# SyncE joins the engines whose order is the written one, in an expert stage of seven block products

## The chip, the cores and the metric

One core of a Trainium2 chip runs the kernel. The metric is the device time in microseconds of one execution, as the median over runs. TensorE, VectorE (DVE), ScalarE (ACT), GpSimd (POOL) and SyncE (SP) each work off a queue of instructions in order. SyncE computes nothing here: it issues most of the DMAs.

## The reference

An attention without softmax feeds a mixture of 16 experts in 4 groups:

```python
scores = scale * np.matmul(z, z.transpose(0, 2, 1))      # u, v: 8 x 1856 x 256, z: 8 x 1856 x 64
attn = np.maximum(scores, 0.0) ** 2
x = (u * np.matmul(attn, v)).reshape(B * S, D)           # 14848 tokens
# each token: the best group by x @ w_group, the best of its 4 experts by x @ w_expert[g]
h = np.maximum(xg[mask_e] @ w1[g, e], 0.0)               # 256 -> 1024
out[tok_idx] = (g_w * e_w)[:, None] * (h @ w2[g, e])     # 1024 -> 256
```

All of it is computed to nearly float32 accuracy: each operand is split in a high and a low part, and each product is three matmuls.

## The kernel before

The attention takes the first 900 us and is not touched. Its tokens are written into a table in DRAM, `bucket`, sorted by expert. The experts are then taken in the order of their load. The first four are computed in the plain way. The last twelve, numbers 4 to 15, are computed each in two halves of at most 512 tokens, which share weights: phase 1 (`x @ w1`) uses seven block products where the plain way has eight. This stage runs from about 957 us to the end, and the change touches it alone.

For one expert `e` the program writes down this work:

- The product loop: 28 products of phase 1 (`step`, matmuls at L1318), 4 of which run already in the phase 2 of the expert before. With 20 left it calls `duo_rows(e + 1)`, which asks for the next expert's tokens: two register loads on SyncE for the expert's number and row (`regs`, L742 and L743), two transposing DMAs from `bucket` into `xp_w` (L1240), and two small loads of `meta_w` (L1247), the tokens' weights and places. With 8 left it calls `duo_w1(e + 1)`, two loads of 512 KB into the buffers `r0` and `r1` (L1182). Between products GpSimd splits this expert's `w2` out of the same two buffers (L1227, L1228).
- Phase 2 of the first half, `phase2_t(f"w{e}_0", ...)`: 48 matmuls (L871) in two sweeps. By the plan `A`, ScalarE and VectorE meanwhile split the next expert's `w1` (L1194, L1204, L1208 to L1211), then `duo_w2(e + 1)` loads its `w2` into `r0` and `r1` (L1188), then VectorE joins the next expert's tokens out of `xp_w` (L1261). At the end of each sweep ScalarE moves the result from PSUM to `yp_w` (L874, L879). At the end SyncE issues four transposing DMAs from `yp_w` to `yr_w` (L884).
- Phase 2 of the second half, `phase2_t(f"w{e}_1", ...)`, in the same way. By the plan `B`, the first four products of the next expert run among its matmuls, beginning in the second sweep (`1 11 go; 1 12 m; ...`). Among them is product 1, which ScalarE copies from PSUM to `duo_y` (L1336); products 6 and 2 are added on top.
- A result is sent by tiles of 128 tokens: a copy out of `yr_w` by ScalarE (L906) or VectorE (L910), a multiplication with the token's weight (L908, L913), and an indirect DMA by GpSimd (L914). The letters `sa`, `sv` in the plans and `send_part` in the product loop say when. By `B`, the two first tiles of an expert's first half are sent at `1 3 sv` and `1 8 sa`, in the second sweep of its second half, ahead of `1 11 go`.

Buffers: `xp_w` has 2, `meta_w` 7, `yr_w` 4, `yp_w` 2.

What sets the order: the program text is traced, and a scheduler arranges each engine's queue from it, unless told otherwise. Inside `tc.manual_schedule(engines=...)` the engines named keep the order in which the text was written. Around the twelve experts it names TensorE, ScalarE and VectorE. SyncE and GpSimd are arranged by the scheduler there: an instruction of a later expert may stand ahead of one of an earlier expert. Each instruction still waits for its data and buffers. The region opens before the first of the twelve experts' product loops and closes before the last half of the last one.

Of the kernel before, what the change touches and what calls it, by code (L numbers as in the profile page):

```python
# [29 lines left out]
def tile_glu_attn_moe(  # L30
# [1401 lines left out]
    while unsent:  # L1432
        unsent.pop(0)()
    in_order = ExitStack()
    in_order.enter_context(tc.manual_schedule(
        engines={mybir.EngineType.PE, mybir.EngineType.Activation, mybir.EngineType.DVE}
    ))
    sending = []

# [141 lines left out]
```

## Time and profile before

| | us |
|---|---|
| median of 3 runs | 1445.79 (1445.42 to 1455.44) |
| the profiled execution's own time | 1446.41 |
| its span, first to last instruction | 1444.5 |
| TensorE busy | 1420.8 (98%) |
| VectorE busy | 1214.9 (84%) |
| ScalarE busy | 1052.2 (73%) |
| GpSimd busy | 441.6 (31%) |

The clock column of a table of stretches is TensorE's granted clock as a share of full speed, a mean over the stretch. Matmuls are pipelined, so TensorE counts as busy also where it isn't at its peak. A row in a timeline gives the start, the time taken, the engine, the line of the program, the operation, what was written and read, and, in square brackets, how long the engine was idle just before and what ended that.

### The profile page before, as it was taken

How to read it: one execution, taken by the hardware profiler on the slowest of the kernel's cores; microseconds unless marked ns; L12 is line 12 of the kernel's file. 1: busy time of each engine (PE TensorE's matmuls, PEld its weight loads, DVE VectorE, ACT ScalarE, POOL GpSimd, SP SyncE). 2: the span in 40 equal slices, each digit the busy share in tenths (PEclk: the TensorE clock that was granted, in tenths of full speed). 3: DMA queues.
4: the chain of work that ended last, by engine and by line, in shares of the span. 5: the costliest groups of instructions: out<-in, count | busy, mean ns of one | idle time of the engine just before them, and what ended most of it. 6: DMA issues, size and time to landing. Idle time of an engine off the chain costs nothing.

```text
span 1444.5 us, 22598 instructions
## 1 busy us (share of the span) xinstructions
PE 1420.8 (98%) x6981; PEld 1227.3 (85%) x6981; DVE 1214.9 (84%) x2434; ACT 1052.2 (73%) x1850; POOL 441.6 (31%) x462
## 2 busy tenths in 40 slices
PE   9999999999999999999999999999999999999997
PEld 7898888888888888888788999978788888888896
DVE  7889999999998999989988578787787788678783
ACT  8897888787878878878775344456677777677674
POOL 0002012220222202221114222242445555555564
PEclk9999999999999999999999999999999999999999
DMA  9987969979699798995975464635444545545441
GB/s 320 336 236 210 253 169 258 235 212 225 178 261 227 195 235 189 263 235 149 247 184 154 95 184 77 148 86 120 119 120 111 136 121 129 131 133 131 121 116 52
DMA packets 400045, 256.47 MB, mean 178 GB/s; under 512 B 244132, under 2 KB 355263, under 8 KB 399921
## 3 DMA queue, kind: packets, MB, share of 16 engines
q1 hardware_dynamic: 387984, 223.97, 62.9%
q0 software_dynamic: 11856, 30.90, 6.9%
q8 instruction: 55, 0.90, 0.3%
q14 instruction: 70, 0.57, 0.1%
q10 hardware_dynamic: 80, 0.13, 0.0%
HBM read 108.29 MB, written 89.21 MB: 137 GB/s over the span
## 4 chain that ended last, share of the span: by engine, by line
PE 83%; DVE 9%; issue 3%; DMA 2%; ACT 2%; POOL 1%; SPq 0%; POOLq 0%; DVEq 0%; ACTq 0%
PE o L403 14%; PE o L404 14%; PE o L406 13%; PE yT L871 7%; PE duo_p L871 7%; PE duo_y L1318 5%; PE sc L366 5%; PE sc L367 5%; PE ph L794 2%; PE ph L795 2%; PE ph L796 2%; PE duo_x L1318 2%; PE duo_w L1318 2%; PE duo_p L1318 2%; DMA yr_w<-yp_w 2%
## 5 line engine op out<-in xcount | busy, mean ns | idle before, releaser
L403 PE MATMUL o<-ah,vl 128*128 128x512 f32 (+2 forms) x960 | 354.4, 370 | 0.6 <-DVE ah L378 0.4
L404 PE MATMUL o<-ah,vh 128*128 128x512 f32 (+2 forms) x960 | 354.3, 369 | 0.0
L406 PE MATMUL o<-al,vh 128*128 128x512 f32 (+2 forms) x896 | 329.0, 369 | 0.0
L638 POOL DMA_INDIRECT bucket<-rows,di x121 | 137.5, 1137 | 376.0 <-issue 216.6
L370 ACT ACTIVATE r<-sc 128x512 f32<-128x512 f32 (+2 forms) x312 | 178.7, 573 | 82.7 <-PE sc L367 77.7
L403 PEld LDWEIGHTS o<-ah,vl 128*128 128x128 f32 x960 | 180.2, 188 | 30.8 <-DVE ah L378 0.8
L914 POOL DMA_INDIRECT out_dram<-y_w,meta_w x92 | 148.6, 1615 | 188.8 <-ACT y_w L908 167.0
L404 PEld LDWEIGHTS o<-ah,vh 128*128 128x128 f32 x960 | 180.2, 188 | 29.0
L381 DVE TENSOR_TENSOR al<-r,ah 128x512 fp32r<-128x512 f32 (+2 forms) x280 | 187.9, 671 | 17.3 <-DVE ah L378 0.5
L406 PEld LDWEIGHTS o<-al,vh 128*128 128x128 f32 x896 | 167.9, 188 | 26.6 <-DVE al L381 0.7
L871 PE MATMUL duo_p<-hh_w,duo_w 128*128 128x496 f32 (+9 forms) x692 | 182.2, 377 | 0.0
L377 ACT ACTIVATE r<-r 128x512 f32<-128x512 f32 (+2 forms) x284 | 173.9, 612 | 9.0
L871 PEld LDWEIGHTS duo_p<-hh_w,duo_w 128*128 128x128 f32 x692 | 130.7, 189 | 17.3
L378 DVE CAST ah<-r 128x512 fp32r<-128x512 f32 (+2 forms) x284 | 117.7, 414 | 22.0 <-ACT r L377 15.1
L366 PE MATMUL sc<-zm,z2h 128*128 128x512 f32 (+2 forms) x312 | 120.1, 385 | 0.4 <-ACT vh L289 0.4
L367 PE MATMUL sc<-zm,z2l 128*128 128x512 f32 (+2 forms) x312 | 118.9, 381 | 0.0
L871 PE MATMUL duo_p<-hl_w,duo_w 128*128 128x496 f32 (+9 forms) x346 | 105.9, 376 | 0.0
L306 DVE STREAM_TRANSPOSE mt<-r 128x512 f32<-128x512 f32 x147 | 103.7, 705 | 0.6
L356 DVE TENSOR_TENSOR al<-at,ah 128x512 fp32r<-128x512 f32 (+1 forms) x168 | 95.3, 579 | 3.1 <-ACT ah L355 3.0
L355 ACT CAST ah<-at 128x512 fp32r<-128x512 f32 (+1 forms) x168 | 86.1, 532 | 7.7 <-DMA sym<-mt 4.6
L871 PE MATMUL yT<-hh,w_e 128*128 128x512 f32 (+6 forms) x384 | 83.3, 333 | 0.0
L914 POOL DMA_INDIRECT out_dram<-y,meta x37 | 40.8, 1104 | 120.7 <-DVE y L913 116.8
(237 smaller groups left out, 2862.1 us busy)
## 6 DMA issues: line engine op xcount, KB each, us to landing
sym<-mt SPq DMA_DIRECT2D x126, 256.0 KB
duo_r<-in_w_dram SPq DMA_DIRECT2D x48, 512.0 KB
at<-sym SPq DMA_DIRECT2D x84, 256.0 KB
bucket<-padrow SPq DMA_DIRECT2D x32, 660.0 KB
at<-sym SPq DMA_DIRECT2D x84, 160.0 KB
vr<-in_v_dram SPq DMA_DIRECT2D x23, 512.0 KB
ut<-in_uT_dram SPq DMA_DIRECT2D x23, 512.0 KB
raw_e<-in_w_dram SPq DMA_DIRECT2D x16, 512.0 KB
```

What stands on the lines that cost most here:

```text
L366: held(nc.tensor.matmul(ps[:, 0:w], z2h[:, ks], zm, start=True, stop=False))
L367: held(nc.tensor.matmul(ps[:, 0:w], z2l[:, ks], zm, start=False, stop=True))
L370: held(nc.scalar.activation(out=a, in_=ps[:, 0:w], func=AF.Relu, scale=1.0 / S))
L377: held(nc.scalar.activation(out=a, in_=a, func=AF.Square))
L381: held(nc.vector.tensor_sub(out=al, in0=a, in1=f32(ah)))
L403: held(nc.tensor.matmul(o, vl[:, dsl], ah, start=(i == 0), stop=False))
L404: held(nc.tensor.matmul(o, vh[:, dsl], ah, start=False, stop=end and al is None))
L406: held(nc.tensor.matmul(o, vh[:, dsl], al, start=False, stop=end))
L638: nc.gpsimd.indirect_dma_start(out=views[(b * NQ + 2 * half + hs[h]) * NT + i], out_offset=bass.IndirectOffsetOnAxis(ap=di[0:n, i0 + i:i0 ...
L871: nc.tensor.matmul(o, wt["2"][f // 2][:, w0:w0 + P], hs[f][q // 2][:, 0:n], start=(at == 0), stop=(at == 3 * NF - 1))
L914: nc.gpsimd.indirect_dma_start(out=outs(), out_offset=bass.IndirectOffsetOnAxis(ap=meta[0:m, t, 1:2], axis=0), in_=y[0:m], in_offset=None, ...
L1318: nc.tensor.matmul(out, a, b, start=(q == 0 and m in (1, 5)), stop=(q == 2), skip_group_check=True)
```

## The change

SyncE is named too. No instruction, buffer or size is changed.

```diff
@@ -1433,7 +1433,7 @@
         unsent.pop(0)()
     in_order = ExitStack()
     in_order.enter_context(tc.manual_schedule(
-        engines={mybir.EngineType.PE, mybir.EngineType.Activation, mybir.EngineType.DVE}
+        engines={mybir.EngineType.PE, mybir.EngineType.Activation, mybir.EngineType.DVE, mybir.EngineType.SP}
     ))
     sending = []
```

## Rows read from the trace of the kernel before

**Rows 1.** The page, section 1: engine, busy us, share of span, instructions.

```profile
PE 1420.8 (98%) x6981; PEld 1227.3 (85%) x6981; DVE 1214.9 (84%) x2434; ACT 1052.2 (73%) x1850; POOL 441.6 (31%) x462
```

**Rows 2.** Stretches, one per expert: length, engines' busy us, clock; ten and their sum.

```profile
1017.70:1062.00 44.30, 42.31 (x181) 34.80 (x180) 32.94 (x51) 30.30 (x50) 19.95 (x18) 0.96 0.48 118
...
1220.70:1264.00 43.30, 40.48 (x181) 35.88 (x181) 31.48 (x51) 29.09 (x50) 21.54 (x18) 0.92 0.51 117
...
1340.50:1379.80 39.30, 37.40 (x183) 34.99 (x181) 30.19 (x51) 27.85 (x50) 22.05 (x18) 0.96 0.50 130
1379.80:1415.30 35.50, 35.50 (x181) 33.73 (x180) 30.92 (x51) 28.23 (x50) 22.11 (x17) 1.00 0.34 94
sum 397.60, PE 387.47 PEld 341.15 DVE 316.91 ACT 291.04 POOL 215.96; mean PE 38.75 PEld 34.11 DVE 31.69 ACT 29.10 POOL 21.60
```

**Rows 3.** Waits of TensorE, 957 to 1444 us: total us, times, longest.

```profile
PE duo_y L1318 <- ACT duo_y L1336: 10.1, 7, 2.8
```

**Rows 4.** Timeline of ScalarE, 1351 to 1363 us, expert 13's phase 2.

```profile
1352.67 0.26 ACT L879 COPY yp_w<-duo_p 128x112 uint16<-128x112 uint16 x1
...
1357.39 0.26 ACT L879 COPY yp_w<-duo_p 128x112 uint16<-128x112 uint16 x1
1360.67 0.76 ACT L906 COPY y_w<-yr_w 128x512 uint16<-128x512 uint16 x1 [3.02 <-DMA yr_w<-yp_w]
...
1361.88 0.50 ACT L1336 COPY duo_y<-duo_x 128x424 f32<-128x424 f32 x1
```

**Rows 5.** Timeline of TensorE, the matmul behind that copy.

```profile
1362.43 0.92 PE L1318 MATMUL duo_y<-duo_x,duo_t 128*128 128x424 f32 x3 [1.90 <-ACT duo_y L1336]
```

**Rows 6.** Timeline of SyncE's queue, 1346 to 1380 us: issues, their time on the queue.

```profile
1346.80 2.55 SPq L1188 DMA_DIRECT2D duo_r<-in_w_dram  x2
1349.69 4.15 SPq L1247 DMA_DIRECT2D meta_w<-bucket  x2
1354.04 2.11 SPq L1240 DMA_TRANSPOSE xp_w<-bucket  x1
1356.26 5.14 SPq L884 DMA_TRANSPOSE yr_w<-yp_w  x4
1361.58 1.44 SPq L1240 DMA_TRANSPOSE xp_w<-bucket  x1
1367.47 5.42 SPq L884 DMA_TRANSPOSE yr_w<-yp_w  x4
1373.15 5.08 SPq L1182 DMA_DIRECT2D duo_r<-in_w_dram  x2
```

**Rows 7.** Waits of SyncE's queue, 957 to 1400 us: total us, times, longest.

```profile
SPq L1182 <- POOL duo_w L1228: 60.2, 12, 8.1
SPq L1247 <- DMA out_dram<-y_w,meta_w: 28.3, 9, 3.6
```

**Rows 8.** Timelines, 1392 to 1400 us, expert 14: SyncE's queue, ScalarE, VectorE, TensorE.

```profile
1392.00 40.50 SPq L884 DMA_TRANSPOSE yr_w<-yp_w  x12
...
1396.95 0.79 ACT L906 COPY y_w<-yr_w 128x512 uint16<-128x512 uint16 x1
...
1395.18 3.63 DVE L1194 TENSOR_TENSOR duo_x<-duo_r,duo_x 128x448 fp32r<-128x448 f32 x4
...
1399.09 0.77 PE L1318 MATMUL duo_y<-duo_x,duo_t 128*128 128x448 f32 x3
```

**Rows 9.** Register loads of an expert's number: ns min/median/max, first and last start.

```profile
L742 SPq TENSOR_LOAD <-eli x16: 262/269/496, 727.1 to 829.1; - x16
L742 SPq FUSED_REGOPS  x16: 147/147/187, 727.7 to 829.4; - x16
```

**Rows 10.** DMA, 1373 to 1385 us, 40 slices of 0.3 us; then ScalarE, VectorE.

```profile
GB/s 277 101 0 82 82 137 137 123 273 410 396 260 191 96 0 0 0 0 0 109 137 273 218 259 341 205 205 0 0 55 0 0 27 0 0 0 0 0 0 0
...
1381.36 0.62 ACT L1204 CAST duo_p<-duo_r 128x512 fp32r<-128x512 f32 x1
...
1382.72 0.69 DVE L1209 TENSOR_TENSOR duo_r<-duo_r,duo_r 128x512 f32<-128x512 f32 x1
```

## The prediction

> **What bounds the kernel now.** I read the page first, then the last third of the span by expert, then the waits of TensorE there, then the queue that feeds the engine it waits for.
>
> The page: TensorE is busy for 98% of the span [rows 1]. So a change pays only where it removes time in which TensorE stands still or runs slowly. The change touches the last stage alone (from about 957 us on), the experts computed by seven block products.
>
> The table by expert shows how much that is. Ten stretches, each from one expert's first output matmul to the next expert's, make 397.60 us, and TensorE is busy for 387.47 of them: 10.1 us idle [rows 2]. In three stretches the granted clock falls below 1.00, to 0.96, 0.92 and 0.96; in the other seven it is 1.00, as in the last one shown. The clock has two levels, 2.4 and 1.2 GHz, so a mean of 0.92 over 43.30 us means 3.5 us lost; the three together lose 0.04 x 44.30 + 0.08 x 43.30 + 0.04 x 39.30 = 6.8 us. The two with the longest waits are among them. The stage thus loses 10.1 + 6.8 = 16.9 us.
>
> The waits give one cause for all of the idle time: the matmul of L1318 into `duo_y` waits for ScalarE's copy L1336, 10.1 us in 7 waits, at most 2.8 [rows 3]. That copy itself takes 0.50 us. It is late because ScalarE's order is fixed and a copy of L906 stands ahead of it, which waited 3.02 us for a DMA, the transposes of `yr_w`; ScalarE had been free since 1357.65 [rows 4]. TensorE got its operand at 1362.43, after 1.90 us without work [rows 5].
>
> Why is that DMA late? The order of SyncE's queue tells [rows 6]. The `yr_w` transposes (L884) begin at 1356.26. Their input was complete at 1352.93, when the eviction L879 of the first half ended [rows 4]; that is 3.3 us earlier. Ahead of them stand two `meta_w` loads (4.15 us) and one `xp_w` transpose (2.11 us), which belong to the expert after next. The loads are long because they wait for scatters: 28.3 us in 9 waits [rows 7], 3.1 on average.
>
> **The change part by part.** It adds SyncE to the engines kept in the written order. No instruction is added or removed. In the written order, per expert, the queue holds `w1` (L1182), `w2` (L1188), `yr` of the first half, `yr` of the second half (L884), and then, in the next expert's product loop, `xp` twice (L1240), `meta` twice (L1247), and that loop's `w1`. Against rows 6, the two `meta` and two `xp` move from around the first `yr` to behind the second `yr`, ahead of `w1`. Also, the two register loads of `regs` (L742, L743), which now all run before 830 us [rows 9], come into the stage, ahead of the first `xp`.
>
> *What it gives.* The first `yr` starts when its input is there, 3.3 us earlier for the expert of rows 4 and 6. The trace has this case already: the expert whose `yr` starts at 1392.00 has no later expert's rows to fetch, so its queue is in the written order. There L906 runs at 1396.95 with no idle time before it, the matmul starts at 1399.09 with none either, and its stretch, the last of the ten, has clock 1.00 and no idle time [rows 2, 8]. It is also the shortest stretch, 35.50 us, with the least work of TensorE to hide behind. So I take all of the 10.1 us, and with them the 6.8 us of clock, as the clock fell only in stretches with such a wait: -16.9.
>
> *What the moved instructions cost in the new place.* The `xp` rows are first read by L1261, which the plan puts behind the whole split of `w1`, so they have more room than `w1` behind them, and that sets the price. Its delay per expert: register loads 2 x (0.27 + 0.15 + 0.02), about 1.1 with the gaps [rows 9]; `xp` 2.11 + 1.44 [rows 6]; two `meta` without the wait 4.15 - 3.1 = 1.0; gaps of about 0.2 each, 0.7: sum 6.3 us. The tightest is the last expert: the first `w1` load is issued at 1373.15, its bytes have come by about 1376.8 (the slices from the fourth to the thirteenth), and it is first read at 1381.36, 4.5 us later; the second has come at about 1381.1 (the twenty-seventh slice) and is read at 1382.72 [rows 6, 10]. Delayed by 6.3, the first lands at about 1383.1, 1.7 late. The second is held today not by the queue but by GpSimd, which must have read the buffer (L1182 waits for L1228, 5.0 us on average [rows 7]); it follows the first at the 400 GB/s of the fullest slices [rows 10], 512 KB in 1.3 us, and lands at about 1384.4, 1.7 late. VectorE then runs on without a pause to the matmul of 1399.09, with 0.28 us to spare (1395.18 + 3.63 against 1399.09) [rows 8]. So the last expert loses about 1.5 us. Wider experts have longer product loops and so more room: the first stretch without its idle time and clock loss is 44.30 - 1.99 - 1.77 = 40.5 us, against 35.5 for the last [rows 2]. I take nothing for them. The bounds: 0, if the loads overlap better, and 10 x 1.5 = 15 us, if all are as tight as the last. I take 1.5, as only the last has so little slack.
>
> The Trainium skill puts the floor of such a register load at about 0.6 us (DMA: Bandwidth & Descriptors, section Latency and other measured facts). The rows show a median of 0.27 [rows 9], so the trace is lower; by the page the delay of `w1` would be 0.7 us longer and the sum 0.7 us worse.
>
> What would have covered the wait of `meta`: by the new place the scatters it waited for are an expert's half older, so I cost it at nothing; if that cover is gone it costs what the second rival says. The order of TensorE, ScalarE and VectorE is fixed before and after. GpSimd's is not, and may be arranged anew; the rows give no sign of which way.
>
> *Sum.* 1446.4 (the profiled execution; span 1444.5) - 16.9 + 1.5 = 1431.0. The median of the runs shown is 0.6 us lower, which makes 1430.4; I say 1430.
>
> **Rivals.**
>
> 1. *Weight loads late for all.* `w1` slips past its slack in every expert, not only the last. For it: second loads that already land 1.6 us before their reader [rows 10]. Against: the wider experts' longer loops. Price: 10 x 1.5 = 15 us, so 1446.4 - 16.9 + 15 - 0.6 = 1444. The Trainium skill says that on each DMA engine descriptors are consumed in ring order (DMA: Bandwidth & Descriptors, section Queues, rings and completion order); by that, `w1` would also wait for the bytes of `xp` ahead of it, and this rival would come true. No row here shows `w1` behind `xp`.
>
> 2. *A new wait (the one that ends slower).* The `meta` loads keep their wait for a scatter in the new place, at 3.1 us, and `w1` queues behind them. The delay is then 9.4 us, and each of ten experts starts its weight work about 3.1 us late: 31 us, and if each wait costs clock as the three of rows 2 do (6.8 / 3 = 2.3), 23 more. On the sum above, 1430.4, that gives 1461 to 1484. It decides from a delay of about 8 us on. For it: 9 such waits today. Against: the buffers come from a set of seven, two per expert, and the scatters of the expert before last are over by then.
>
> 3. *The transposes stay late.* `yr` starts earlier but lands no sooner, as the second `w2` load is still moving when it starts, and half of the wait and of the clock loss stays: 1446.4 - 8.5 - 0.6 + 1.5 = 1439. Against: rows 8, where `w2` stands directly ahead too.
>
> 4. *The order hardly changes*, or TensorE finds another wait at the same place: 1446. Rows 6 are not the written order, so something must move; and rows 3 name no second cause.
>
> **How the numbers follow.** Forecast 0.60 (1427 to 1434), rival 1: 0.14, rival 2: 0.07, rival 3: 0.13, rival 4: 0.06. A measurement of this kernel can tell about 1% from no change, which is 14.5 us; the border is 1431.3. The forecast lies just past it, so I give 0.51 to faster (most of the forecast's 0.60), 0.42 to within 1% (the rest of it and rivals 1, 3 and 4), and 0.07 to slower. The lower end is 1427: all of the 16.9 with nothing lost is 1428.9, and the clock column's rounding (0.005 of 126.9 us) and its edges may hide a microsecond or two. The upper end, for 8 in 10, is 1442: it takes in the forecast and rival 3, and leaves out rivals 2 and 4 and most of 1.
>
> **What would show it.** Right: in SyncE's queue `yr_w` of the first half directly behind `w2`; no wait of L1318 for L1336; ScalarE's L906 with no idle time ahead of it; granted clock 1.00 in all ten stretches. The cost would show as a wait of ScalarE's L1204 or VectorE's L1208 or L1209 for the DMA of `duo_r`, in the last expert or two. Wrong: such waits from the first experts on, a wait of L1247 ahead of L1182, or a `duo_y` wait that stays.

## The result, and the profile after

The changed kernel takes 1436.11 us (median, 1435.32 to 1438.14), the kernel before 1447.63 us in the same measurement. The ratio is 0.9917, with a 95% interval of 0.9896 to 0.9939: 11.5 us or 0.8% faster, against a forecast of 16. That is inside the range and on the right side, but just under the 1% that the prediction took as the border. Among the executions of the kernel before that were measured with the first four experiments, one took 1554.99 us at a granted clock of 0.85; the ratios leave it out, and 1443.08 us below is the median with it (1442.25 without).

The profiled execution took 1438.14 us, with a span of 1436.1; it is the slowest of the seven. I compare it with that of before in the order of the prediction.

**The queue.** SyncE's queue for the same stretch as [rows 6] (start us, time on the queue, operation, count):

```profile
1338.50 2.55 SPq L1188 DMA_DIRECT2D duo_r<-in_w_dram  x2
1344.51 15.55 SPq L884 DMA_TRANSPOSE yr_w<-yp_w  x8
1361.40 3.89 SPq L1240 DMA_TRANSPOSE xp_w<-bucket  x2
1365.63 1.11 SPq L1247 DMA_DIRECT2D meta_w<-bucket  x2
1367.00 0.94 SPq L1182 DMA_DIRECT2D duo_r<-in_w_dram  x2
```

It is the written order: `w2`, both halves' `yr`, `xp`, `meta`, `w1`. The `meta` loads take 1.11 us instead of 4.15. The price stands in the same rows: the last `yr` ends at 1344.51 + 15.55 = 1360.06, and `w1` is issued at 1367.00, 6.9 us later. Before, it followed after 0.3 [rows 6].

**The wait that was to go.** ScalarE and TensorE at the place of [rows 4, 5] (the first copy ends the first half, whose `yr` are then issued):

```profile
1344.38 0.26 ACT L879 COPY yp_w<-duo_p 128x112 uint16<-128x112 uint16 x1
...
1349.24 0.80 ACT L906 COPY y_w<-yr_w 128x512 uint16<-128x512 uint16 x1
...
1350.49 0.51 ACT L1336 COPY duo_y<-duo_x 128x424 f32<-128x424 f32 x1
```

```profile
1351.53 0.74 PE L1318 MATMUL duo_y<-duo_x,duo_t 128*128 128x424 f32 x3
```

No idle time stands ahead of any of them. The 3.02 us of ScalarE and the 1.90 us of TensorE are gone here. ScalarE's waits for `yr_w` over the whole stage, before and after (total us, times, longest):

```profile
ACT y_w L906 <- DMA yr_w<-yp_w: 29.7, 11, 4.5
ACT y_w L906 <- DMA yr_w<-yp_w: 3.5, 2, 2.3
```

The two that are left come behind the ten stretches, at 1420.96 and 1423.60 us, and two such stood there before the change as well. In the view of TensorE's waits from 950 us on, no wait for L1336 is left. What stands there instead is this:

```profile
PE duo_p L871 <- ACT hh_w L1326: 4.5, 3, 2.9
```

**The wait that came.** L1326 is ScalarE's eviction of a phase 1 product, here the expert's last (`M4` in the plan `A`). It does not touch the weights. ScalarE in the last such case, and TensorE beside it:

```profile
1368.38 0.52 ACT L1326 ACTIVATE hh_w<-duo_z 128x424 fp32r<-128x424 f32 x1
1372.51 0.62 ACT L1204 CAST duo_p<-duo_r 128x512 fp32r<-128x512 f32 x1 [3.62 <-DMA duo_r<-in_w_dram]
1373.04 0.52 ACT L1326 ACTIVATE hh_w<-duo_y 128x424 fp32r<-128x424 f32 x1
```

```profile
1368.66 2.09 PE L871 MATMUL duo_p<-hh_w,duo_w 128*128 128x424 f32 x10
1373.61 1.08 PE L871 MATMUL duo_p<-hh_w,duo_w 128*128 128x424 f32 x2 [2.86 <-ACT hh_w L1326]
1374.48 2.73 PE L871 MATMUL duo_p<-hl_w,duo_w 128*128 128x424 f32 x8
```

The cast L1204, the first reader of the next expert's `w1`, stands ahead of that eviction in ScalarE's order. It waits 3.62 us for the load; the eviction behind it can't pass; TensorE waits 2.86 us for the eviction. The difference, 0.76 us, is the slack of this place. The third row also shows the clock after that wait: eight matmuls in 2.73 us, about 0.34 each, where the same matmuls at full clock start 0.2 apart. The granted clock from 1374 to 1376 us is 0.50, the lower of the two levels; from 1368.66 to 1370.75 us, ahead of the wait, it is 1.00.

ScalarE's waits for these loads, over the whole stage:

```profile
ACT duo_p L1204 <- DMA duo_r<-in_w_dram: 9.0, 7, 3.6
```

VectorE waits for them too, 4.7 us in 3 waits at L1208 and 4.3 us in 7 at L1209. SyncE's `meta` loads wait for scatters for 0.9 us in 4 waits.

**By expert.** The ten stretches, as [rows 2] (length, busy us of PE, PEld, DVE, ACT, POOL, clock, DMA share, GB/s); six like the first row, ahead of it, are left out:

```profile
1256.02:1293.24 37.22, 37.22 (x181) 33.58 (x180) 31.25 (x51) 28.68 (x50) 22.50 (x18) 1.00 0.52 128
1293.24:1331.13 37.89, 36.60 (x182) 33.62 (x180) 31.07 (x51) 28.39 (x50) 22.43 (x18) 1.00 0.54 136
1331.13:1367.21 36.08, 35.77 (x181) 33.60 (x180) 30.34 (x51) 27.88 (x50) 22.19 (x18) 1.00 0.54 138
1367.21:1407.05 39.84, 36.98 (x182) 34.91 (x180) 31.14 (x51) 28.44 (x50) 22.11 (x17) 0.96 0.44 102
sum 386.28, PE 381.81 PEld 337.94 DVE 318.78 ACT 292.10 POOL 218.64; mean PE 38.18 PEld 33.79 DVE 31.88 ACT 29.21 POOL 21.86
```

The sum is 386.28 against 397.60: 11.3 us less. The first seven have no idle time at all and a clock of 1.00. The last three have 1.29, 0.31 and 2.86 us, and the last, which was the shortest of the ten before with 35.50, is now 39.84, with a clock of 0.96. So the stage won more than 11.3 and lost part of it in three experts.

In the first of these three, `w1` came later than in the others:

```profile
1291.11 1.92 SPq L1247 DMA_DIRECT2D meta_w<-bucket  x2
1293.30 0.95 SPq L1182 DMA_DIRECT2D duo_r<-in_w_dram  x2
```

The `meta` issues took 1.92 us instead of 1.11 there, and `w1` followed the last `yr` after 7.8 us, where the other nine stretches have 6.7 to 7.7. The second profile of the same kernel shows it at the same place (2.26 and 7.9 us). The queue's waits name no cause for it, and no run tests it.

Of these 11.3 us the span shows 8.4 (1444.5 to 1436.1), because the first stretch begins at 1020.77 instead of 1017.70. Whether this has to do with the change is a question for the runs.

### The profile page after: what moved, and what is told of

Read it like the earlier page. It is cut to its first block, busy times and chain, and to the rows that moved or that the text cites. A ratio compares the mean times of both kernels' runs of the same rounds, so it can differ in the third digit from the quotient of the medians.

```text
span 1436.1 us, 22571 instructions
## 1 busy us (share of the span) xinstructions
PE 1416.2 (99%) x6981; PEld 1223.4 (85%) x6981; DVE 1214.1 (85%) x2434; ACT 1048.2 (73%) x1850; POOL 441.2 (31%) x462
## 4 chain that ended last, share of the span: by engine, by line
PE 88%; DMA 3%; issue 2%; DVE 2%; SPq 2%; ACT 2%; POOL 1%; POOLq 0%; ACTq 0%; DVEq 0%
PE duo_p L871 15%; PE o L403 12%; PE o L404 12%; PE o L406 12%; PE yT L871 7%; PE duo_y L1318 5%; PE sc L366 4%; PE sc L367 4%; PE ph L794 2%; PE ph L795 2%; PE ph L796 2%; PE duo_x L1318 2%; PE duo_w L1318 2%; PE duo_p L1318 2%; PE duo_z L1318 1%
```

## The experiments

**Theory A:** the change wins what the prediction said, and loses because `w1`, issued about 7 us later, keeps ScalarE and then TensorE waiting in the last experts. **Theory B:** the 3 us by which the stage began later belong to the change as well. Four kernels were run against one measurement of the kernel before (1443.08 us).

**The changed kernel once more**, with no edit.

> The changed kernel once more, for a second profile. Theory A (the gain that is missing went into weight loads that land late): about 1436 us, with some 4.5 us of TensorE waits for ScalarE's hh_w in the last three experts. Theory B (3 us went ahead of the stage: in the first profile of the changed kernel TensorE was 3.1 us later than before at every matmul from 753 us on): the shift is there again, the stage's first matmul near 959.8 us and not near 956.7. Under A alone the shift is chance and may be absent.

Measured 1433.17 us (1432.08 to 1435.83), ratio 0.9931 [0.9910, 0.9952]. The first and last of its stretches, the sum, and TensorE's wait:

```profile
1017.74:1058.34 40.60, 40.60 (x181) 33.78 (x180) 33.31 (x51) 30.49 (x50) 20.22 (x18) 1.00 0.50 131
...
1364.35:1401.95 37.60, 36.09 (x181) 33.58 (x180) 31.13 (x51) 28.36 (x50) 22.11 (x17) 1.00 0.38 108
sum 384.21, PE 381.07 PEld 336.81 DVE 318.25 ACT 291.98 POOL 217.40; mean PE 38.11 PEld 33.68 DVE 31.83 ACT 29.20 POOL 21.74
```

```profile
PE duo_p L871 <- ACT hh_w L1326: 3.1, 3, 1.5
```

The stage begins at 1017.74, as before the change: Theory B falls, the 3 us of the first profile were not the change's; all eight later profiles, each with SyncE in the written order, begin the stage's first stretch between 1017.2 and 1018.4 us. The wait is there again, in the same three experts, 3.1 instead of 4.5 us, and no stretch shows a clock below 1.00 here.

**`w1` ahead of the next expert's rows.** The loads are asked for in the order `w1`, then `xp` and `meta`, in the same place of the product loop:

```diff
-            if more and len(prods) == 20:
-                duo_rows(e + 1)
             if more and len(prods) == 8:
                 duo_w1(e + 1)
+                duo_rows(e + 1)
```

> The next expert's w1 loads are written ahead of its rows, so SyncE's queue has w1, then xp and meta. Theory A: the waits of ScalarE and VectorE for the DMA of duo_r go, and with them TensorE's waits for hh_w (4.5 us and about 1.5 us of clock): about 1430 us. Theory B: no change, about 1436. If the rows are now the late ones, VectorE waits for xp_w and the time is between.

Measured 1428.30 us (1427.71 to 1429.70), ratio 0.9894 [0.9869, 0.9919], 4.9 us below the changed kernel beside it. Its queue, ScalarE at the cast, and the last stretch with the sum:

```profile
1339.58 16.04 SPq L884 DMA_TRANSPOSE yr_w<-yp_w  x8
1357.09 4.01 SPq L1182 DMA_DIRECT2D duo_r<-in_w_dram  x2
1361.23 4.84 SPq L1240 DMA_TRANSPOSE xp_w<-bucket  x2
1366.41 1.67 SPq L1247 DMA_DIRECT2D meta_w<-bucket  x2
```

```profile
1364.38 0.62 ACT L1204 CAST duo_p<-duo_r 128x512 fp32r<-128x512 f32 x1
1364.89 0.54 ACT L1326 ACTIVATE hh_w<-duo_y 128x424 fp32r<-128x424 f32 x1
```

```profile
1362.81:1398.35 35.54, 35.54 (x182) 33.74 (x181) 30.94 (x51) 28.24 (x50) 22.12 (x17) 1.00 0.53 121
sum 379.93, PE 379.83 PEld 337.07 DVE 317.29 ACT 291.35 POOL 217.21; mean PE 37.98 PEld 33.71 DVE 31.73 ACT 29.14 POOL 21.72
```

`w1` is issued 1.5 us after the last `yr` (1357.09 against 1355.62) instead of 6.9, the cast has no idle time ahead of it, and all ten stretches have a clock of 1.00. The stage shows 0.1 us of idle time in 379.93. So the ten stretches can give 397.60 - 379.93 = 17.7 us; the changed kernel's 386.28 leaves 6.4 of that, the second profile's 384.21 leaves 4.3.

**The register loads ahead of the stage.** They are 1.3 us of the delay:

```diff
+    for e in range(NOLD, NE):
+        regs(e)
     in_order = ExitStack()
```

> The register loads of all twelve experts are written ahead of the stage, so that in the stage w1 stands 1.3 us earlier on SyncE. Theory A: waits in the expert before last and the one ahead of it go, the last shrinks from 3.0 to about 1.7 us: 1433. Theory B: the loads run before 830 us again as in the kernel before; the stage begins near 956.7 us, about 1433 too, but with hh_w waits of 3 us or more in its profile.

Measured 1429.11 us (1428.45 to 1430.13), ratio 0.9902 [0.9877, 0.9927]. The queue, and what is left of ScalarE's wait:

```profile
1338.75 15.91 SPq L884 DMA_TRANSPOSE yr_w<-yp_w  x8
1354.79 3.76 SPq L1240 DMA_TRANSPOSE xp_w<-bucket  x2
1358.88 1.09 SPq L1247 DMA_DIRECT2D meta_w<-bucket  x2
1360.23 0.95 SPq L1182 DMA_DIRECT2D duo_r<-in_w_dram  x2
```

```profile
ACT duo_p L1204 <- DMA duo_r<-in_w_dram: 1.3, 2, 0.8
```

`w1` is issued 5.6 us after the last `yr`, 1.3 earlier than in the changed kernel. This is a miss of the size that was expected: 1.3 us per expert gave 4.1 in all, nearly as much as the whole cure. The lateness of the changed kernel thus lay just past the point where it begins to cost: 1.3 us less in each of three experts removes waits of 3.1 us in all, 1.5 at most.

**The cast behind the eviction.** The load stays late, but ScalarE's and VectorE's first steps of the split stand behind `M4`:

```diff
-        A = ("0 0 p S3 S1; 0 4 M4; 0 5 s S2 S4; 0 8 a pl; ..."
+        A = ("0 4 M4; 0 5 p S3 S1 s S2 S4; 0 8 a pl; ..."
```

> In plan A the first work on the new w1 (p, S3, S1) comes behind product 4 of the old expert, so that ScalarE and VectorE first finish the old expert's hidden values. If lateness reaches TensorE because ScalarE's p stands ahead of an eviction that TensorE needs: the hh_w waits go and the time is about 1432. If it reaches TensorE through VectorE's chain to product 6, as the prediction had it: the loss stays, as waits at duo_y, about 1436.

Measured 1431.59 us (1430.81 to 1432.17), ratio 0.9919 [0.9894, 0.9944]. TensorE's waits, and ScalarE's in the last case:

```profile
PE duo_w L1318 <- DVE duo_x L1194: 0.7, 1, 0.7
PE duo_p L871 <- ACT yp_w L879: 0.4, 1, 0.4
PE duo_x L1318 <- DVE duo_x L1194: 0.3, 1, 0.3
```

```profile
1364.01 0.53 ACT L1326 ACTIVATE hh_w<-duo_y 128x424 fp32r<-128x424 f32 x1
1366.72 0.62 ACT L1204 CAST duo_p<-duo_r 128x512 fp32r<-128x512 f32 x1 [2.19 <-DMA duo_r<-in_w_dram]
```

The cast waits as long as in the changed kernel's second profile (2.22 us there), yet no L1326 keeps TensorE waiting any more. So it is the order behind the cast that carries this wait over. The edit moves ScalarE's and VectorE's steps together; that ScalarE's is the one that counts is read from the trace of the changed kernel, where L1326 ends TensorE's wait, and was not tested by itself. 1.6 us are won of the 4.9 that `w1` first wins. What the profile names for the rest is small waits of TensorE, 1.0 us of them for VectorE's split (L1194): the path that the prediction had priced comes second. The edit itself also begins that split later, so how much of the rest the changed kernel already had isn't shown.

For the gain itself a dose was still missing. **Rival C:** it came from elsewhere in the new order, not from the place of the first half's `yr`. Theory A says that it is this place and nothing else. Four more kernels ran against another measurement of before (1443.17 us).

**The rows ahead of the first half's `yr`.** The rows of the expert after next are asked for at the end of the first half's plan, so that `xp` and `meta` stand ahead of `yr` again, now in every expert, with SyncE in the written order:

```diff
-            if more and len(prods) == 20:
+            if e == NOLD and len(prods) == 20:
                 duo_rows(e + 1)
...
+        do["rows"] = lambda: duo_rows(e + 2) if e + 2 < NE else None
...
-             "... 1 16 sv x2; 1 20 T1 T3")
+             "... 1 16 sv x2; 1 20 T1 T3 rows")
```

> SyncE stays in the written order, but the program now asks for the rows of the expert after next (the xp_w transposes and the meta_w loads) at the end of the first half's plan, so they stand ahead of the first half's yr_w transposes, as several of them did before the change. The w1 loads then follow the second half's yr_w directly. Theory A (the gain of the change is the place of the first yr_w, and nothing else): the yr_w transposes start 5 us or more after their input is there, L906 waits for them again, L1336 behind it, and the wait of L1318 for L1336 comes back in most experts, larger than the 10.1 us of the kernel before: 30 us or more, with the clock below 1.00 in these stretches; time 1465 to 1500. No wait of L1326, as w1 is early. Rival C (the gain came from elsewhere in the queue's order, and L906 is not what TensorE waits for): within 5 us of the changed kernel, 1430 to 1438.

Measured 1465.21 us (1461.13 to 1466.84), ratio 1.0142 [1.0118, 1.0166]. TensorE's wait, the queue, ScalarE, and two of the stretches with the sum of all ten:

```profile
PE duo_y L1318 <- ACT duo_y L1336: 23.3, 9, 3.2
```

```profile
1371.45 4.08 SPq L1240 DMA_TRANSPOSE xp_w<-bucket  x2
1375.87 1.17 SPq L1247 DMA_DIRECT2D meta_w<-bucket  x2
1377.09 15.56 SPq L884 DMA_TRANSPOSE yr_w<-yp_w  x8
```

```profile
1380.80 0.77 ACT L906 COPY y_w<-yr_w 128x512 uint16<-128x512 uint16 x1 [4.27 <-DMA yr_w<-yp_w]
...
1382.01 0.51 ACT L1336 COPY duo_y<-duo_x 128x424 f32<-128x424 f32 x1
```

```profile
1063.15:1107.31 44.16, 42.13 (x181) 34.84 (x180) 33.11 (x51) 30.31 (x50) 20.68 (x18) 0.96 0.44 118
...
1192.04:1232.83 40.79, 38.49 (x181) 33.57 (x180) 31.83 (x51) 29.20 (x50) 21.45 (x18) 1.00 0.46 122
...
sum 417.26, PE 393.98 PEld 346.10 DVE 317.00 ACT 291.39 POOL 215.28; mean PE 39.40 PEld 34.61 DVE 31.70 ACT 29.14 POOL 21.53
```

The wait of [rows 3] is back, in nine stretches instead of seven and 23.3 us instead of 10.1, and seven stretches have a clock below 1.00 (0.96 in six that make 255.5 us, 0.92 in one of 43.7). 0.04 x 255.5 + 0.08 x 43.7 = 13.7 us of clock and 23.3 of idle time make 37.0; the sum is 37.3 above that of the version without waits. The idle time is less than the 30 us expected, the time at the low end. Rival C falls.

**The rows between the two halves' `yr`.** The call stands behind the first half's `phase2_t`:

```diff
-            if more and len(prods) == 20:
+            if e == NOLD and len(prods) == 20:
                 duo_rows(e + 1)
...
+        if e + 2 < NE:
+            duo_rows(e + 2)
         if more:
             unsent += phase2_t(f"w{e}_1", ...
```

> As the run before, but the rows stand between the first half's yr_w and the second half's, so the first yr_w keeps the place that the change gave it and w1 stands directly behind the second yr_w. Theory A: no wait of L1318 for L1336, and no wait of L1326 or L1204 for late weights either; the second half's yr_w have their readers only in the next product loop and can bear some microseconds: 1427 to 1431, like the version with w1 ahead of the rows. Rival C: as the changed kernel, 1433 to 1436; a third possibility, that the second half's yr_w now come late, would show as a wait of L906 or L910 for yr_w in the product loop and give 1435 or more.

Measured 1428.39 us (1427.94 to 1429.60), ratio 0.9899 [0.9879, 0.9918], with neither wait of TensorE. The second half's `yr` bear the delay.

**Both cures together**, `w1` first and the register loads early.

> Both cures together: w1 asked for ahead of the next expert's rows, and the register loads made ahead of the stage. Theory A (the lateness of w1 is the whole loss, and either cure alone already ends it): no further gain, within 1 us of the version with w1 ahead of the rows alone, 1427 to 1429. Rival D (the register loads cost something by themselves, 24 loads at about 0.3 to 0.5 us in SyncE's order): 3 us or more below it, 1424 to 1426.

Measured 1428.40 us (1427.77 to 1428.75), ratio 0.9897 [0.9879, 0.9916]. Nothing is added, so the register loads cost only through the lateness of `w1`: Rival D, that they cost something by themselves, falls.

**`w1` first once more**, to compare with.

> The version with w1 ahead of the rows again, on the same chip as the three others, to compare with: 1428 within 1.5 us, and no wait of L1326 by TensorE in the stage.

Measured 1428.37 us (1427.78 to 1428.70), ratio 0.9895 [0.9876, 0.9913]. Three orders of the queue that serve both readers in time end at 1428.4. They are 1.0 to 1.1% faster than the kernel before and 4.9 us below the changed kernel where the two were measured together.

## Why the prediction was right, and which term was mis-sized

**What bounds the kernel, and the cause of the wait.** Right, each link: `yr` directly behind `w2`, L906 and L1336 without idle time, TensorE's wait gone. The run with the rows ahead turns it round: the same wait comes back by putting the same loads in the same place.

**What it gives, 16.9 us.** Right in size. The ten stretches without any of the waits are 17.7 us shorter than before. The prediction's two parts were 10.1 us of idle time and 6.8 of clock; that the clock comes back with the wait was an inference from three stretches, and it held: in the four profiles read by expert (the two of the change, `w1` first, the rows ahead) no stretch shows less than 1.00 without a wait of TensorE in it.

**The delay of `w1`, 6.3 us.** Nearly right: 6.9 - 0.3 = 6.6 to 6.7. The parts were `xp` 3.55 (measured 3.89), `meta` 1.0 (1.11), the register loads 1.1 (1.3 between the last `yr` and the first `xp`), gaps 0.7. A register load itself took this in the stage:

```profile
L742 SPq TENSOR_LOAD <-eli x10: 288/296/304, 1011.4 to 1360.1; - x10
```

So the row of before (269 ns) was the right price. The Trainium skill (DMA: Bandwidth & Descriptors, section Latency and other measured facts) gives about 600 ns as a floor; the trace shows half.

**What the delay costs, 1.5 us.** This is the term that was mis-sized: 6.4 us in the first profile, 4.3 in the second, 4.9 between the medians measured together. Three steps that led to it failed.

- *The path.* The prediction let the late load run through VectorE's chain to the matmul of product 6, which had 0.28 us to spare. But the cast L1204 also stands in ScalarE's fixed order, ahead of the eviction of `M4`, for which TensorE has 0.76 us to spare (3.62 - 2.86). The nearest work behind a waiting instruction is what comes next on the same engine, whether or not it reads the same data. The prediction had used this very argument for L906 and L1336, and did not ask it of L1204.
- *How many experts.* It took nothing for all but the last, because the first stretch is 40.5 us wide without its losses and the last 35.5. The stretches between were not put in that row. The one before the last is 39.30 - 1.9 - 0.04 x 39.30 = 35.8 us [rows 2], as narrow as the last. Three experts lost, by 1.5, 0.6 and 4.3 us of stretch against the version with `w1` first. The width doesn't decide alone: the first of the three is wider than the second and lost more, with `w1` 7.8 us behind the last `yr` instead of 6.8.
- *The clock.* No clock was charged for the new wait. In the first profile it cost 0.04 x 39.84 = 1.6 us; in the second no stretch shows it.

The forecast of 1.7 us of lateness for the last expert's first load was itself short. ScalarE's cast waited 3.62 us in the first profile and 2.22 in the second. What differs is how the loads land; the page's GB/s of DMA in 40 slices, first the profile of the change (1364 to 1374 us), then its second (1362 to 1371):

```profile
GB/s 142 276 289 292 278 274 180 187 93 228 292 263 30 3 6 53 68 246 147 229 246 262 360 361 344 393 410 328 361 262 49 49 33 33 16 33 16 0 0 0
```

```profile
GB/s 289 290 234 259 180 208 38 243 290 290 87 10 8 3 167 74 55 164 182 291 419 273 510 328 473 382 419 382 273 364 18 0 0 0 0 0 0 0 0 0
```

In the first, the two loads end in a tail of some 1.7 us at 16 to 49 GB/s, where 262 to 410 stood just before; in the second there is none. What made the tail is not shown.

**The rivals.** Rival 1 (weight loads late for all) is what happened in mechanism but not in extent: ScalarE waited for the load in 7 experts, TensorE in 3, and the price was 4 to 6 us, not 15. By the Trainium skill's ring order (DMA: Bandwidth & Descriptors, section Queues, rings and completion order) `w1` would also have waited for the bytes of `xp`; the first GB/s row shows that these were through about when `w1` was issued (1367.00): 3 to 6 GB/s at 1367.3 to 1367.7, then the rise. In this expert the delay is that of the queue alone. Rival 2 (`meta` keeps its wait) did not come: 0.9 us in 4 waits, against 28.3 in 9 before [rows 7]. Rival 3 (transposes land no sooner) did not come either: in the ten stretches L906 found its data without a wait. Rival 4 falls with the first table.

**The time.** In the first profile: 1446.4 - 17.7 + 6.4 + 3.1 (the later begin of the stage, by chance) = 1438.2, against 1438.14. This adds up measured terms and only shows that none is left out. With the mis-sized term at its measured 4 to 6 us, the prediction's own sum would have been 1433 to 1435, and the chance of being past the 1% border small.

## What to carry to other kernels

When a DMA queue is put into the written order, sum up what comes to stand ahead of each load, and then, for its first reader on every in-order engine, look at the instruction behind that reader: a late load stops that one too, with all that waits for it. Take the room from every stretch, not from the widest and the narrowest. And where a queue follows the written order, that order has to be chosen: the loads with the nearest reader go first; here `w1` ahead of the next rows, or the rows between the halves' transposes, gave the last 5 us.

## What the runs showed of the hardware

- The same load had different landings: ScalarE, waiting for it, began 3.95 us after the issue in the second profile (1364.31 to 1368.26) and 5.5 us in the first (1367.00 to 1372.51). The 1.6 us of difference are about the length of the tail at 16 to 49 GB/s (1.7 us).
- Not every wait of TensorE cost clock: waits of 1.5 us (second profile) and 1.29 us left the stretch at 1.00, one of 2.86 us was followed by matmuls about 0.34 us apart instead of 0.2 and a stretch at 0.96. The length alone doesn't tell which: with the rows ahead, a stretch with 40.79 - 38.49 = 2.30 us of idle time stayed at 1.00, and one with 44.16 - 42.13 = 2.03 us fell to 0.96.
- A wait took more than its idle time also where the clock stayed at 1.00: the last stretch of the second profile is 37.60 - 35.54 = 2.06 us longer than with `w1` first, and 37.60 - 36.09 = 1.51 us of it are idle time. Where the other 0.5 us lie is not shown.
